# Linear attention and two MLP layers on one core: phi as the stationary operand of the product with v, v with a column of ones, and the identity matrix made on VectorE

## The chip, the cores and the metric

The kernel runs on one core of a Trainium2 chip. Times are device microseconds (us) from the first to the last instruction of one execution and what lies around them; smaller is better. TensorE (PE, its weight loads PEld) multiplies matrices, VectorE (DVE) and ScalarE (ACT) work element by element, GpSimd (POOL) does what the others can't, and SyncE (SP) issues nearly all DMAs.

## What is computed

The reference, cut to what matters:

```python
# q, k, v: (4, 8, 576, 64)   w_phi: (64, 128)
def phi(x):
    proj = np.einsum('bhsd,df->bhsf', x, w_phi)
    proj = proj - np.max(np.abs(proj), axis=-1, keepdims=True)
    return np.concatenate([np.exp(proj), np.exp(-proj)], axis=-1)
q_p, k_p = (phi(q), phi(k))
kv = np.einsum('bhsf,bhsd->bhfd', k_p, v)
z = np.sum(k_p, axis=2)
num = np.einsum('bhsf,bhfd->bhsd', q_p, kv)
den = np.einsum('bhsf,bhf->bhs', q_p, z)[..., None] + 1e-06
x = num / den                                   # laid out as (2304, 512)
h = x @ w_in;  x = np.maximum(h, 0) ** 2 @ w_out            # d_ff 2048
out = (sigmoid(x @ w_gate) * (x @ w_val)) @ w_out2          # d_ff 1536
```

phi has 256 features for each position of a head: 128 of exp(proj) and 128 of exp(-proj). kv is, for each head, 256 x 64, and z the sum of phi over the positions.

## The kernel before, in words

**Attention** runs in 16 steps, one for each batch b and pair j of heads (e = 0, 1). The 576 positions of a head are four rows r of 128 and a rest of 64; the rests of two heads lie together in the tiles kr, vr and phr. TensorE transposes q and k by the identity matrix (trans_q, L292; trans_k, L285; trans_rem, L300), multiplies them by w_phi (proj_q, L313; proj_k, L334), and the features come from exp on ScalarE. The maximum over the features of q comes from GpSimd's all-reduce (L318), that of k from VectorE (L339). phi of k is the tile ph: 128 positions by r, u and 128 features, where u = 0, 1 is the half of the features.

kv(b, j) makes kv and z with the *positions* contracted. v is the stationary operand and phi the moving one (L360): 64 columns of the array hold v of one head, the other 64 those of the other, and 256 columns of phi pass, so the bank pk has v's 64 dimensions of both heads on its 128 rows. The sums z come from a second row of matmuls (L367) with 32 columns of ones as the stationary operand, in four groups of columns. num(b, j), the product with phi of q, needs the *features* on the rows. So kt is copied out of PSUM (L369, L370), kv_tr transposes it in three pieces (L377), and L379 copies the result to ks. num has a product for the denominators (L390, 32 equal columns of z) and one for the numerators (L397), and VectorE and GpSimd turn these into the quotients (L401 to L417).

Step n issues, in this order: the exponentials of n, the projections of n+1 (L334, L313), the transposes of n+2, kv of n, num of n-1, kv_tr of n, and the loads of n+3. Each engine works in the order in which the scheduler put its instructions. PSUM is a pool of eight banks that all of this shares. Before the first step, make_identity (masks.py) clears a tile and sets its diagonal on GpSimd; TensorE begins with eight warm-up matmuls of the identity (L245).

**Weights.** Between the steps, and in the block that follows, weights arrive as 8-byte words and are converted (weight, L105 to L118: three operations on VectorE, a square on ScalarE, one more on VectorE). convert1(k) does the k-th piece of the first layer's w_in and w_out and writes the result to HBM (L147, L133); ten pieces are converted during attention, the other 22 in the first block, at 7/4 a step.

**The first block of the first layer** (t = 0) has steps s = 0 to 17: h0_step makes 128 columns of the hidden layer (L517) and squares them in two parts, ghi and glo (L521, L523), and o1_step multiplies those by w_out (L538). The further blocks use sums of the pieces of w_in (Strassen's scheme, L590), which in_sums makes: it reads two converted pieces back from HBM (L176, into the tiles wf that the block's own weights use too), forms four sums on VectorE (sums, L163 to L166, one buffer s) and writes them to HBM (L167). It is called for i = 0 to 7 at s = 3, 5, ..., 17.

Of the kernel before, what the change touches and what calls it, by code (L numbers as in the profile page):

```python
# [9 lines left out]

F32 = mybir.dt.float32
# [3 lines left out]
ALU = mybir.AluOpType  # L15
# [5 lines left out]
def attention_moe_moe2(ctx, tc, q, k, v, w_phi, w_in, w_out, w_gate, w_val, w_out2, out):  # L21
# [62 lines left out]
    def col_src(w, c):  # L84
        return w[:, c * P:(c + 1) * P].rearrange("(j p) f -> p j f", p=P)
# [40 lines left out]
    def in_piece(c):  # L126
        q, r = divmod(c, 4)
        return half[2 * q + r % 2][:, r // 2]
# [15 lines left out]
    def convert1(k):  # L144
        o, c = order1[k]
        if o == "in":
            nc.sync.dma_start(out=in_piece(c), in_=weight(wpa, col_src(w_in, c)))  # L147
        else:
            park(("o1", c), weight(wpa, row_src(w_out, c)))
        done.add((o, c))  # L150

    done = set()
    gvd = [dr.tile([P, 2, NJ * P], F32, tag=f"gv{c}", name="gvd") for c in range(C2)]
# [3 lines left out]
    kept = {}  # L157

    def sums(a, b, dst):
        a11, a12, a21, a22 = a[:, :HF], a[:, HF:], b[:, :HF], b[:, HF:]  # L160
# [52 lines left out]
    with ExitStack() as actx:  # L213
# [16 lines left out]
        ones = cst.tile([P, 32], F32, name="ones")  # L230
        nc.vector.memset(ones, 1.0)
# [17 lines left out]
        def load_rem(b):  # L249
            kr = ld.tile([SR, H, D], F32, tag="kr", name="kr", bufs=1)  # L250
            nc.sync.dma_start(out=kr, in_=k[b, :, SM:S, :].rearrange("h p d -> p h d"))
            nat["kr", b] = kr
            vr = lv.tile([P, 2, 2, D], F32, tag="vr", name="vr", bufs=2)
            for a in range(2):
                nc.sync.dma_start(out=vr[a * SR:(a + 1) * SR].rearrange("p g e d -> p (g e) d"),
                                  in_=v[b, 4 * a:4 * a + 4, SM:S, :].rearrange("h p d -> p h d"))
            nat["vr", b] = vr

        def load(b, j):
            t = ld.tile([P96, 2, 6, D], F32, tag="q", name="q", bufs=3)  # L260
            nc.sync.dma_start(out=t, in_=q[b, 2 * j:2 * j + 2].rearrange("h (p r) d -> p h r d", r=6))
            nat["q", b, j] = t
            t = ld.tile([P, 2, 4, D], F32, tag="k", name="k", bufs=3)
            nc.sync.dma_start(
                out=t, in_=k[b, 2 * j:2 * j + 2, 0:SM, :].rearrange("h (p r) d -> p h r d", r=4))
            nat["k", b, j] = t
            t = lv.tile([P, 2, 4, D], F32, tag="vx", name="vx", bufs=3)
            nc.sync.dma_start(
                out=t, in_=v[b, 2 * j:2 * j + 2, 0:SM, :].rearrange("h (p r) d -> p h r d", r=4))
            nat["vx", b, j] = t  # L270

        tT = {}
# [70 lines left out]
            ph[key] = t  # L343

        kvs = {}
        kts = {}


        def kv(b, j):
            tr = ph["r", b]  # L350
            vx = nat["vx", b, j]
            vr = nat["vr", b]
            a, g = divmod(j, 2)
            sl = slice(a * SR, (a + 1) * SR)
            pk = bank(2 * F)
            pz = bank(F)
            for r in range(5):
                for e in range(2):
# [3 lines left out]
            for r in range(5):  # L362
                for e in range(2):
                    l, t = (ones, ph[b, 2 * j + e][:, r]) if r < 4 else (ones[sl], tr[sl, 2 * g + e])
# [3 lines left out]
            kt = sm.tile([P, 3, F], F32, tag="kvt", name="kvt", bufs=2)  # L368
            nc.scalar.activation(kt[:, 0:2].rearrange("p u f -> p (u f)"), pk, AF.Copy)  # L369
            nc.scalar.activation(kt[:, 2], pz, AF.Copy)  # L370
            kts[b, j] = kt

        def kv_tr(b, j):
            kt = kts[b, j]
            pt = bank(3 * P)
            for u in range(3):
                nc.tensor.transpose(pt[:, u * P:(u + 1) * P], kt[:, u], ident)  # L377
            ks = sm.tile([P, 3 * P], F32, tag="kvs", name="kvs", bufs=3)
            nc.scalar.activation(ks, pt, AF.Copy)  # L379
            kvs[b, j] = ks  # L380

        def num(b, j):
            ks = kvs[b, j]
            pd = bank(SH)
            for u in range(2):
                for e in range(2):
                    for i in range(2):
                        q = 32 * (2 * e + i)
                        o = 2 * P + 32 * (2 * e + u)
                        nc.tensor.matmul(pd[q:q + 32], lhsT=ks[:, o:o + 32], rhs=qx[b, 2 * j + e, i][:, u, :],  # L390
                                         start=u == 0, stop=u == 1)
            pn = [bank(SH) for i in range(2)]
            for i in range(2):
                for u in range(2):
                    for e in range(2):
                        o = u * P + e * D
# [58 lines left out]
        for n in range(B * NJ):  # L455
# [331 lines left out]
    for s in range(C1 + 2):  # L787
        if s < C1:
            fetch_for(s + ahead)
            h0_step(s)  # L790
            split_in(s + 1)
        if 1 <= s <= C1:
            split_out(s - 1)
        for i, k in ((C1 - 5, "B11"), (C1 - 4, "B21"), (C1 - 3, "T2"), (C1 - 1, "T3"), (C1 - 1, "T1"), (C1, "B22"), (C1, "T4")):
            if s == i:
                xop(1, k)
        if s >= C1 - 1:
            run_ahead(0, 5, 0 if s < C1 else 3)
        if s >= 2:
            o1_step(0, s - 2, ws.pop(("out", s - 2)))  # L800
        if s < C1:
            converts1(s)
        if s >= 3 and s % 2 and s <= C1 + 1:
            for i in range(C1 // 2):
                if i == (s - 3) // 2:
                    in_sums(i)

    for k, (at, fn, *args) in enumerate(acts):
        run_ahead(first[k], 11, 6)
        fn(*args)  # L810
        converts2(at)
# [30 lines left out]
```

## Time and profile before

| | |
|---|---|
| median of 3 runs | 1026.83 us (1023.62 to 1028.88) |
| profiled execution, own time | 1027.08 us |
| its span, first to last instruction | 1025.3 us |
| PE busy | 992.4 us (97%) |
| PEld / DVE / ACT / POOL busy | 870.3 / 746.6 / 601.0 / 109.4 us |
| mean granted clock of TensorE | 0.994 |
| DMA moved | 162.18 MB, mean 158 GB/s |

The profile is of one execution. Attention takes the first 204 us, the first block of the first layer the time to about 343 us, and the other blocks of both layers the rest. "Busy" is the time in which an engine worked on at least one instruction; TensorE's matmuls are pipelined and their ends modelled. "Idle before" is the time that an engine stood still before an instruction, with what ended it. The chain of work that ended last is followed back from the last instruction: at each step to what released it. The granted clock is a share of full speed.

### The profile page before, as it was taken

The numbers are of one execution on the slowest core, as the hardware profiler recorded it, in microseconds if no ns is written. First come the engines' busy times: TensorE is split into PE (matmuls) and PEld (weight loads), VectorE is DVE, ScalarE is ACT, GpSimd is POOL, SyncE is SP. The second block draws the span as 40 slices with busy tenths as digits, with TensorE's granted clock in tenths as the row PEclk, the third lists the DMA queues.
The fourth block names the chain that finished last, engine by engine and source line by source line (L and its number), as shares of the span: only waits on it lengthen the run. The fifth ranks groups of instructions, "written<-read, shape, count | busy, mean of one in ns | idle before, by whom it ended". The sixth has DMA issues, their size and how long they took to land.

```text
span 1025.3 us, 17544 instructions
## 1 busy us (share of the span) xinstructions
PE 992.4 (97%) x6488; PEld 870.3 (85%) x6488; DVE 746.6 (73%) x1283; ACT 601.0 (59%) x1081; POOL 109.4 (11%) x198
## 2 busy tenths in 40 slices
PE   5999999999999899999999999999999999999996
PEld 5666666599999799889998899998899988899985
DVE  4799999869875797887968869866566656566542
ACT  4988888546545487545875457654465544455431
POOL 3555665400000000000000000000000000000000
PEclk9999999999999899999999999999999999999999
DMA  8345421339876478457584565642354422544302
GB/s 225 103 142 153 144 92 46 124 119 352 286 270 211 160 246 267 154 167 243 187 282 160 175 187 175 198 139 73 89 158 133 125 93 62 154 133 124 103 13 61
DMA packets 117846, 162.18 MB, mean 158 GB/s; under 512 B 12928, under 2 KB 75008, under 8 KB 117760
## 3 DMA queue, kind: packets, MB, share of 16 engines
q1 hardware_dynamic: 117120, 160.20, 49.8%
q8 instruction: 51, 0.84, 0.3%
q10 hardware_dynamic: 640, 0.85, 0.2%
q14 instruction: 35, 0.29, 0.1%
HBM read 127.99 MB, written 33.03 MB: 157 GB/s over the span
## 4 chain that ended last, share of the span: by engine, by line
PE 85%; DVE 6%; DMA 4%; ACT 2%; issue 2%; POOL 0%; ACTq 0%; SPq 0%; POOLq 0%; DVEq 0%
PE d L590 37%; PE d L538 17%; PE d L694 15%; PE d L517 4%; PE a L360 3%; DMA wf<-wid 2%; PE a L397 2%; PE a L334 2%; PE a L367 1%; PE a L390 1%; PE a L313 1%; DMA st<-in_moe_w_in_dram 1%; PE a L292 1%; DVE km L339 1%; PE a L377 1%
## 5 line engine op out<-in xcount | busy, mean ns | idle before, releaser
L590 PE MATMUL d<-xs,hl 128*128 128x384 f32 x2184 | 385.5, 337 | 3.6 <-ACT c L596 3.6
L590 PEld LDWEIGHTS d<-xs,hl 128*128 128x128 f32 x2184 | 379.5, 188 | 6.7 <-ACT c L596 4.9
L139 DVE TENSOR_TENSOR hl<-wf,hl 128x512 fp32r<-128x512 f32 x282 | 192.5, 688 | 76.4 <-ACT hl L138 75.3
L138 ACT ACTIVATE hl<-wf 128x512 fp32r<-128x512 f32 x282 | 174.9, 625 | 94.4 <-PE d L590 47.5
L538 PE MATMUL d<-ghi,hl 128*128 128x256 f32 (+1 forms) x768 | 191.9, 340 | 0.0
L538 PEld LDWEIGHTS d<-ghi,hl 128*128 128x128 f32 x768 | 133.0, 190 | 16.4
L538 PE MATMUL d<-glo,hl 128*128 128x512 f32 (+1 forms) x384 | 130.0, 342 | 5.1 <-DVE glo L523 5.1
L694 PE MATMUL d<-hl,ghi 128*128 128x512 f32 x432 | 126.7, 395 | 0.0
L94 ACT ACTIVATE ghi<-G 128x768 fp32r<-128x768 f32 x48 | 40.7, 847 | 99.3 <-PE d L694 56.0
L694 PEld LDWEIGHTS d<-hl,ghi 128*128 128x128 f32 x432 | 80.9, 188 | 18.2
L97 DVE TENSOR_TENSOR glo<-G,ghi 128x768 fp32r<-128x768 f32 x48 | 46.0, 958 | 57.3 <-ACT ghi L94 56.9
L596 ACT ACTIVATE c<-d 128x768 f32<-128x768 f32 x78 | 61.3, 809 | 44.7 <-PE d L590 44.5
L318 POOL PARTITION_ALL_REDUCE m<-qe x64 | 82.5, 1359 | 28.5 <-ACT qe L316 26.8
L538 PEld LDWEIGHTS d<-glo,hl 128*128 128x128 f32 x384 | 73.1, 190 | 14.1 <-DVE glo L523 5.4
L619 DVE TENSOR_TENSOR c<-c,d 128x768 f32<-128x768 f32 x54 | 51.2, 953 | 41.1 <-ACT c L596 26.8
L694 PE MATMUL d<-hl,glo 128*128 128x512 f32 x216 | 76.3, 395 | 0.0
L517 PE MATMUL d<-xs,hl 128*128 128x384 f32 x384 | 69.2, 337 | 2.1 <-DVE u L417 1.7
L517 PEld LDWEIGHTS d<-xs,hl 128*128 128x128 f32 x384 | 66.6, 188 | 3.8 <-DVE u L417 2.2
L116 ACT ACTIVATE st<-st 128x512 f32<-128x512 f32 x68 | 45.7, 680 | 37.0 <-DVE w L113 34.2
L694 PEld LDWEIGHTS d<-hl,glo 128*128 128x128 f32 x216 | 40.6, 188 | 9.8
L113 DVE SCALAR_TENSOR_TENSOR w<-st,w 128x512 uint32<-128x512 uint32 x68 | 48.0, 718 | 0.3
L117 DVE SCALAR_TENSOR_TENSOR w<-st,w 128x512 f32<-128x512 f32 x68 | 46.3, 687 | 1.4 <-ACT st L116 0.5
(105 smaller groups left out, 1128.3 us busy)
## 6 DMA issues: line engine op xcount, KB each, us to landing
wf<-wd SPq DMA_DIRECT2D x84, 256.0 KB, 3.0
wf<-smd SPq DMA_DIRECT2D x72, 256.0 KB, 3.0
st<-in_moe_w_out_dram SPq DMA_DIRECT2D x28, 512.0 KB, 5.0
wf<-wid SPq DMA_DIRECT2D x56, 256.0 KB, 4.6
wf<-gvd SPq DMA_DIRECT2D x54, 256.0 KB, 3.1
st<-in_moe_w_in_dram SPq DMA_DIRECT2D x16, 512.0 KB, 5.1
wf<-ismd SPq DMA_DIRECT2D x32, 256.0 KB, 3.5
wd<-w SPq DMA_DIRECT2D x28, 256.0 KB, 3.3
```

Of the source, the lines that this page charges most:

```text
L97: last_g[0] = nc.vector.tensor_tensor(lo, src, f(hi), ALU.subtract)
L113: nc.vector.scalar_tensor_tensor(b, hi, 0xC0000000, b, ALU.bitwise_and, ALU.bitwise_or)
L117: nc.vector.scalar_tensor_tensor(a, h, TINY, a, ALU.is_ge, ALU.mult)
L138: nc.scalar.activation(d[:, 0], a, AF.Copy)
L139: nc.vector.tensor_tensor(d[:, 1], a, f(d[:, 0]), ALU.subtract)
L318: nc.gpsimd.partition_all_reduce(m, a[:, 1, :], channels=P, reduce_op=bass_isa.ReduceOp.absmax)
L517: nc.tensor.matmul(pp[:, i, :n], lhsT=w[:, x, j, :], rhs=xs[j][:, y, o:o + n], start=k == 0, stop=k == 3 * NJ - 1)
L538: nc.tensor.matmul(acc[j][i], lhsT=w[:, x, j, :], rhs=a[y][:, o:o + n], start=c == 0 and k == 0 and (i == 0 or j % 2 == 0), stop=c == C1 - ...
L590: nc.tensor.matmul(acc[k, q][:, m], lhsT=w[:, i, 2 * m + kt, :], rhs=v[:, j, kt, :], start=start and n == 0, stop=n == 5, skip_group_check ...
L596: nc.scalar.activation(side[name, q], acc["X", q], AF.Copy)
L619: nc.vector.tensor_tensor(a, a, acc[k, q], ALU.add)
L694: nc.tensor.matmul(acc[u], lhsT=g[x][:, u * P:(u + 1) * P], rhs=w[:, y].rearrange("p j f -> p (j f)"), start=c == 0 and n == 0, stop=c == ...
```

## The change

kv takes phi as the stationary operand, 128 positions by 128 features, and v as the moving one: 64 dimensions and a column of ones, 65 columns. The result has the features on its rows at once, kv in 64 columns and z in the 65th, for each head e and half u: one bank of 4 x 65 columns, 20 matmuls, one copy to ks. kv_tr, the product with ones and the two copies to kt are gone; num reads z with a step of 0 as 32 equal columns. For the ones, the tiles vx and vr get a 65th column, which GpSimd fills after each allocation, so v's DMAs write 256 bytes at a time, and vx has one DMA for each head. The identity comes from VectorE: a ramp by doubling, its transpose, a comparison, and four copies of a 32 x 32 block. And convert1 makes the sums of two pieces of w_in straight from the converted tiles, for the pieces that are converted after attention (five of the eight pairs); in_sums is called for the other three, at s = 2, 4 and 6.

```diff
     def convert1(k):
         o, c = order1[k]
         if o == "in":
-            nc.sync.dma_start(out=in_piece(c), in_=weight(wpa, col_src(w_in, c)))
+            a = weight(wpa, col_src(w_in, c))
+            nc.sync.dma_start(out=in_piece(c), in_=a)
+            kept[c] = a
+            if k >= len(CONVERTING) and c % 2:
+                sums(kept[c - 1], a, wsm[c // 4][:, :, c % 4 // 2])
+                done.add(("sum", c // 2))
...
         ident = cst.tile([P, P], F32, name="ident")
-        make_identity(nc, ident)
+        ramp = cst.tile([P, 3, 32], F32, name="ramp")
+        nc.vector.memset(ident, 0.0)
+        nc.vector.memset(ramp[:, 0, 0:1], 0.0)
+        for n in (1, 2, 4, 8, 16):
+            nc.vector.tensor_scalar(ramp[:, 0, n:2 * n], ramp[:, 0, :n], float(n), None, ALU.add)
+        nc.vector.transpose(ramp[:, 1], ramp[:, 0])
+        nc.vector.tensor_tensor(ramp[:, 2], ramp[:, 0], ramp[:, 1], ALU.is_equal)
+        for i in range(4):
+            sl = slice(32 * i, 32 * i + 32)
+            nc.vector.tensor_copy(ident[sl, sl], ramp[sl, 2])
...
-            t = lv.tile([P, 2, 4, D], F32, tag="vx", name="vx", bufs=3)
-            nc.sync.dma_start(
-                out=t, in_=v[b, 2 * j:2 * j + 2, 0:SM, :].rearrange("h (p r) d -> p h r d", r=4))
+            t = lv.tile([P, 2, 4, D + 1], F32, tag="vx", name="vx", bufs=3)
+            nc.gpsimd.memset(t[:, :, :, D:], 1.0)
+            for e in range(2):
+                nc.sync.dma_start(
+                    out=t[:, e, :, :D], in_=v[b, 2 * j + e, 0:SM, :].rearrange("(p r) d -> p r d", r=4))
...
-            pk = bank(2 * F)
-            pz = bank(F)
+            pk = bank(4 * (D + 1)).rearrange("p (e u d) -> p e u d", e=2, u=2)
             for r in range(5):
                 for e in range(2):
-                    l, t = (vx[:, e, r, :], ph[b, 2 * j + e][:, r]) if r < 4 else (vr[sl, g, e, :], tr[sl, 2 * g + e])
-                    nc.tensor.matmul(pk[e * D:(e + 1) * D], lhsT=l, rhs=t.rearrange("p u f -> p (u f)"),
-                                     start=r == 0, stop=r == 4)
...
                     for u in range(2):
-                        o = 32 * (2 * e + u)
-                        nc.tensor.matmul(pz[o:o + 32], lhsT=l, rhs=t[:, u], start=r == 0, stop=r == 4)
...
-        def kv_tr(b, j):
...
-                nc.tensor.transpose(pt[:, u * P:(u + 1) * P], kt[:, u], ident)
-            ks = sm.tile([P, 3 * P], F32, tag="kvs", name="kvs", bufs=3)
-            nc.scalar.activation(ks, pt, AF.Copy)
+                        l, t = (ph[b, 2 * j + e][:, r, u], vx[:, e, r]) if r < 4 else (tr[sl, 2 * g + e, u], vr[sl, g, e])
+                        nc.tensor.matmul(pk[:, e, u], lhsT=l, rhs=t, start=r + e + u == 0, stop=r == 4, skip_group_check=True)
+            ks = sm.tile([P, 2, 2, D + 1], F32, tag="kvs", name="kvs", bufs=3)
+            nc.scalar.activation(ks, pk, AF.Copy)
...
-                        nc.tensor.matmul(pd[q:q + 32], lhsT=ks[:, o:o + 32], rhs=qx[b, 2 * j + e, i][:, u, :],
+                        nc.tensor.matmul(pd[q:q + 32], lhsT=ks[:, e, u, D:].to_broadcast([P, 32]), rhs=qx[b, 2 * j + e, i][:, u, :],
...
-                        nc.tensor.matmul(pn[i][e * D:(e + 1) * D], lhsT=ks[:, o:o + D],
+                        nc.tensor.matmul(pn[i][e * D:(e + 1) * D], lhsT=ks[:, e, u, :D],
...
-            kv_tr(b, j)
...
-        if s >= 3 and s % 2 and s <= C1 + 1:
-            for i in range(C1 // 2):
-                if i == (s - 3) // 2:
-                    in_sums(i)
-
+        if s in (2, 4, 6, 8) and ("sum", s // 2 - 1) not in done:
+            in_sums(s // 2 - 1)
```

The order of instructions shows two places. The first is TensorE in one whole attention step, here the kernel before, from the transposes of one step to those of the next (a is a PSUM bank; a matmul here is two instructions in the profile, a transpose one):

```order
L292 MATMUL a<-ident,q 128x96 x6
L285 MATMUL a<-ident,k 128x128 x4
L360 MATMUL a<-ph,vx 64x256 x8
L360 MATMUL a<-phr,vr 64x256 x2
L367 MATMUL a<-ph,ones 32x128 x16
L367 MATMUL a<-phr,ones 32x128 x4
L390 MATMUL a<-qe,kvs 32x288 x8
L397 MATMUL a<-qe,kvs 64x288 x8
L377 MATMUL a<-ident,kvt 128x128 x3
L334 MATMUL a<-wk,kT 128x256 x12
L313 MATMUL a<-qT,wq 128x288 x12
```

And the same step of the changed kernel, whose line numbers differ (L306 and L299 transpose q and k, L371 is kv, L383 and L389 are num, L348 and L327 the projections):

```order
L306 MATMUL a<-ident,q 128x96 x6
L299 MATMUL a<-ident,k 128x128 x4
L371 MATMUL a<-vx,ph 128x65 x16
L371 MATMUL a<-vr,phr 128x65 x4
L383 MATMUL a<-qe,kvs 32x288 x8
L389 MATMUL a<-qe,kvs 64x288 x8
L348 MATMUL a<-wk,kT 128x256 x12
L327 MATMUL a<-qT,wq 128x288 x12
```

The product with ones and the three transposes of kvt are gone, and kv has 20 matmuls with 65 columns in place of 10 with 256.

The second is VectorE at the end of the first block, before (hl and glo are low parts that TensorE waits for, s the sums, c a difference of x for the next block):

```order
L139 TENSOR_TENSOR hl<-wf,hl 128x512
L523 TENSOR_TENSOR glo<-c,ghi 128x768
L139 TENSOR_TENSOR hl<-wf,hl 128x512
L163 TENSOR_TENSOR s<-wf 128x256
L165 TENSOR_TENSOR s<-wf 128x256
L164 TENSOR_TENSOR s<-s,wf 128x256
L166 TENSOR_TENSOR s<-wf,s 128x256
L163 TENSOR_TENSOR s<-wf 128x256
L165 TENSOR_TENSOR s<-wf 128x256
L164 TENSOR_TENSOR s<-s,wf 128x256
L139 TENSOR_TENSOR hl<-wf,hl 128x512
L166 TENSOR_TENSOR s<-wf,s 128x256
```

And the changed kernel around the last glo (L514) of the block:

```order
L138 TENSOR_TENSOR hl<-wf,hl 128x512
L514 TENSOR_TENSOR glo<-c,ghi 128x768
L552 TENSOR_TENSOR c<-u 128x768
L552 TENSOR_TENSOR c<-u,c 128x768
L138 TENSOR_TENSOR hl<-wf,hl 128x512
L96 TENSOR_TENSOR xs<-c,xs 128x768
L138 TENSOR_TENSOR hl<-wf,hl 128x512 x2
L514 TENSOR_TENSOR glo<-c,ghi 128x768
L138 TENSOR_TENSOR hl<-wf,hl 128x512 x2
L514 TENSOR_TENSOR glo<-c,ghi 128x768
L552 TENSOR_TENSOR c<-u 128x768
```

The sums s from wf, between the last two glo before, are no longer there; in the changed kernel they stand earlier, most of them with w, the converted tile, as their source.

## Rows read from the trace of the kernel before

**Rows 1.** By stage: stretch, length, busy PE, PEld, DVE, ACT, POOL; clock, DMA.

```profile
0.00:9.76 9.76, 0.00 (x0) 0.00 (x0) 2.17 (x12) 1.28 (x1) 0.68 (x6) 1.00 0.86 218
...
57.39:138.01 80.62, 80.01 (x918) 52.50 (x917) 75.25 (x166) 68.28 (x168) 47.36 (x85) 1.00 0.49 146
138.01:161.57 23.56, 23.20 (x266) 15.27 (x264) 21.77 (x49) 19.18 (x48) 13.31 (x25) 1.00 0.26 81
...
204.26:343.10 138.84, 133.41 (x759) 124.49 (x759) 100.77 (x177) 70.12 (x104) 0.00 (x0) 0.99 0.72 239
343.10:347.90 4.80, 4.80 (x15) 4.12 (x16) 4.49 (x6) 3.09 (x4) 0.00 (x0) 0.51 0.90 308
```

**Rows 2.** Timeline of the start: start us, us, instruction, count, idle before.

```profile
1.06 0.63 DVE L237 CAST wk<-zr 128x128 fp32r<-128x128 f32 x4
...
9.43 0.28 POOL masks.py:199 TENSOR_SCALAR_AFFINE_SELECT ident<-ident 128x128 f32<-128x128 f32 x1 [8.51 <-issue]
...
9.76 3.74 PE L245 MATMUL a<-ident 128*128 128x128 f32 x16 [9.76 <-POOL ident masks.py:199]
...
13.34 0.66 PE L292 MATMUL a<-ident,q 96*128 96x96 f32 x6
...
16.00 4.95 POOL L318 PARTITION_ALL_REDUCE m<-qe  x4 [6.29 <-ACT qe L316]
```

**Rows 3.** Chain of work that ended last, in one step: start us, us, what.

```profile
68.73 2.46 PE a L360 x20
71.19 1.36 PE a L367 x40
...
75.75 0.48 PE a L377 x3
76.23 1.40 PE a L334 x12
...
79.48 0.49 PE a L285 x4
79.98 2.46 PE a L360 x20
```

**Rows 4.** Timeline at the end of the first block, of DVE and of PE.

```profile
333.83 0.43 DVE L163 TENSOR_TENSOR s<-wf 128x256 f32<-128x256 f32 x1 [4.00 <-DMA wf<-wid]
...
339.54 0.42 DVE L163 TENSOR_TENSOR s<-wf 128x256 f32<-128x256 f32 x1 [4.16 <-DMA ismd<-s]
...
343.10 0.80 PE L538 MATMUL d<-glo,hl 128*128 128x512 f32 x1 [5.07 <-DVE glo L523]
```

**Rows 5.** Groups by form, 0 to 180 us, small DVE operations: busy, mean ns.

```profile
L404 DVE RECIPROCAL rd<-rd 128x9 f32<-128x9 f32 x13 | 2.8, 216 | 0.4
...
L403 DVE TENSOR_SCALAR rd<-den 128x9 f32<-128x9 f32 x13 | 2.1, 163 | 0.1
```

**Rows 6.** DMA issues: KB, median us to landing; last, early q loads.

```profile
vx<-in_v_dram SPq DMA_DIRECT2D x16, 256.0 KB, 3.1
...
vr<-in_v_dram SPq DMA_DIRECT2D x8, 64.0 KB, 2.8
...
DMA to landing us min/median/max: 2.9/4.6/5.9
```

**Rows 7.** Groups by form, 0 to 180 us, weight loads: busy, mean ns.

```profile
L334 PEld LDWEIGHTS a<-wk,kT 128*128 128x128 f32 x180 | 22.4, 188 | 1.8 <-ACT kT L276 1.4 <-DVE kT L277 0.3 <-issue 0.2
...
L360 PEld LDWEIGHTS a<-ph,vx 128*64 128x64 f32 x224 | 14.8, 136 | 8.1 <-ACT qT L276 0.8 <-issue 0.5 <-ACT ph L341 0.3
...
L367 PEld LDWEIGHTS a<-ph,ones 128*32 128x32 f32 x448 | 11.5, 109 | 5.8 <-issue 2.3 <-DVE qT L277 1.5 <-ACT ph L342 0.8
...
L285 PEld LDWEIGHTS a<-ident,k 128*128 128x128 f32 x64 | 6.9, 140 | 0.2
...
L245 PEld LDWEIGHTS a<-ident 128*128 128x128 f32 x16 | 3.5, 330 | 9.8 <-POOL ident masks.py:199 9.8
```

**Rows 8.** Timeline at the end of attention, of PE.

```profile
199.25 1.18 PE L390 MATMUL a<-qe,kvs 128*32 128x288 f32 x16 [0.58 <-ACT kvs L379]
```

More of the change, by code (lines that the diff above doesn't have):

```diff
@@ L6 @@
 from concourse import mybir
-from concourse.masks import make_identity
 from concourse._compat import with_exitstack
@@ L152, in attention_moe_moe2 @@
     done = set()
+    kept = {}
     gvd = [dr.tile([P, 2, NJ * P], F32, tag=f"gv{c}", name="gvd") for c in range(C2)]
@@ L156, in attention_moe_moe2 @@
     order2 += [(c, 2) for c in range(C2)]
-    kept = {}
     def sums(a, b, dst):
@@ L229, in attention_moe_moe2 @@
         split(wq[:, 0], wq[:, 1], wst)
-        ones = cst.tile([P, 32], F32, name="ones")
-        nc.vector.memset(ones, 1.0)
         zr = cst.tile([P, F], F32, name="zr")
@@ L252, in load_rem @@
             nat["kr", b] = kr
-            vr = lv.tile([P, 2, 2, D], F32, tag="vr", name="vr", bufs=2)
+            vr = lv.tile([P, 2, 2, D + 1], F32, tag="vr", name="vr", bufs=2)
+            nc.gpsimd.memset(vr[:, :, :, D:], 1.0)
             for a in range(2):
-                nc.sync.dma_start(out=vr[a * SR:(a + 1) * SR].rearrange("p g e d -> p (g e) d"),
+                nc.sync.dma_start(out=vr[a * SR:(a + 1) * SR, :, :, :D].rearrange("p g e d -> p (g e) d"),
                                   in_=v[b, 4 * a:4 * a + 4, SM:S, :].rearrange("h p d -> p h d"))
@@ L345, in attention_moe_moe2 @@
         kvs = {}
-        kts = {}
         def kv(b, j):
@@ L354, in kv @@
             sl = slice(a * SR, (a + 1) * SR)
-            pk = bank(2 * F)
-            pz = bank(F)
+            pk = bank(4 * (D + 1)).rearrange("p (e u d) -> p e u d", e=2, u=2)
             for r in range(5):
                 for e in range(2):
-                    l, t = (vx[:, e, r, :], ph[b, 2 * j + e][:, r]) if r < 4 else (vr[sl, g, e, :], tr[sl, 2 * g + e])
-                    nc.tensor.matmul(pk[e * D:(e + 1) * D], lhsT=l, rhs=t.rearrange("p u f -> p (u f)"),
-                                     start=r == 0, stop=r == 4)
-            for r in range(5):
-                for e in range(2):
-                    l, t = (ones, ph[b, 2 * j + e][:, r]) if r < 4 else (ones[sl], tr[sl, 2 * g + e])
-                    for u in range(2):
-                        o = 32 * (2 * e + u)
-                        nc.tensor.matmul(pz[o:o + 32], lhsT=l, rhs=t[:, u], start=r == 0, stop=r == 4)
[L368 to L371, printed above, removed]
-        def kv_tr(b, j):
-            kt = kts[b, j]
-            pt = bank(3 * P)
-            for u in range(3):
-                nc.tensor.transpose(pt[:, u * P:(u + 1) * P], kt[:, u], ident)
-            ks = sm.tile([P, 3 * P], F32, tag="kvs", name="kvs", bufs=3)
-            nc.scalar.activation(ks, pt, AF.Copy)
+                    for u in range(2):
+                        l, t = (ph[b, 2 * j + e][:, r, u], vx[:, e, r]) if r < 4 else (tr[sl, 2 * g + e, u], vr[sl, g, e])
+                        nc.tensor.matmul(pk[:, e, u], lhsT=l, rhs=t, start=r + e + u == 0, stop=r == 4, skip_group_check=True)
+            ks = sm.tile([P, 2, 2, D + 1], F32, tag="kvs", name="kvs", bufs=3)
+            nc.scalar.activation(ks, pk, AF.Copy)
             kvs[b, j] = ks
@@ L388, in num @@
                         q = 32 * (2 * e + i)
-                        o = 2 * P + 32 * (2 * e + u)
-                        nc.tensor.matmul(pd[q:q + 32], lhsT=ks[:, o:o + 32], rhs=qx[b, 2 * j + e, i][:, u, :],
+                        nc.tensor.matmul(pd[q:q + 32], lhsT=ks[:, e, u, D:].to_broadcast([P, 32]), rhs=qx[b, 2 * j + e, i][:, u, :],
                                          start=u == 0, stop=u == 1)
@@ L395, in num @@
                     for e in range(2):
-                        o = u * P + e * D
-                        nc.tensor.matmul(pn[i][e * D:(e + 1) * D], lhsT=ks[:, o:o + D],
+                        nc.tensor.matmul(pn[i][e * D:(e + 1) * D], lhsT=ks[:, e, u, :D],
                                          rhs=qx[b, 2 * j + e, i][:, u, :], start=u == 0, stop=u == 1)
@@ L802, in attention_moe_moe2 @@
             converts1(s)
-        if s >= 3 and s % 2 and s <= C1 + 1:
-            for i in range(C1 // 2):
-                if i == (s - 3) // 2:
-                    in_sums(i)
+        if s in (2, 4, 6, 8) and ("sum", s // 2 - 1) not in done:
+            in_sums(s // 2 - 1)
+    kept.clear()
     for k, (at, fn, *args) in enumerate(acts):
```

## The prediction, made before the changed kernel was run

> **What bounds the kernel now.** I read the table by stage first. TensorE is the engine to watch: it idles for the first 9.76 us, is busy 80.01 of 80.62 us in the middle of attention, and 133.41 of 138.84 us in the first block of the first layer [rows 1]. So three places can move: the start, the attention steps and the end of that block. After 347.9 us TensorE has no idle time that this change touches, and I leave that part as it is.
>
> In the timeline of the start TensorE's first instruction, the warm-up of line 245, waits 9.76 us for the identity, which GpSimd finishes with an affine select at 9.43 us after 8.51 us in which nothing that the profile shows ran on it [rows 2].
>
> In the chain of one attention step (head pair) TensorE's own instructions follow each other. From one product with v to the next it is 79.98 - 68.73 = 11.25 us [rows 3]. What TensorE does is then paid in full, unless VectorE ends the step: it is busy 21.77 of 23.56 us in one later stretch [rows 1].
>
> At the end of the block, TensorE's row at 343.10 us shows 5.07 us of idle time before the last product of the block, for the low part glo. VectorE made glo late since it works in order and stood 4.00 and 4.16 us before the sums of lines 163 to 166, once for a piece read back from HBM, once for the buffer that the previous sums were being written from [rows 4]. In the 4.80 us behind that idle time the granted clock is 0.51, the lower of TensorE's levels [rows 1].
>
> **The change, part by part.**
>
> *Start.* Thirteen small VectorE instructions replace the GpSimd pair. The nearest rows are operations on 9 columns, 163 and 216 ns [rows 5]; I take 0.19 us each, 2.5 us. Clearing zr and the four casts of line 237 (0.63 us in all) stand between them, some 0.8 us, so from VectorE's first work at 0.80 us the identity is there at 4.1 us (3.6 to 4.5 by the two rows). The warm-up then takes as long as before, 13.34 - 9.76 = 3.58 us [rows 2], so the first transposes of q stand at 7.7 us and not 13.34. That is **-5.6 us** if nothing else is late. Next in line: the data, and GpSimd's all-reduce. q is there: a load of q lands 2.9 to 5.9 us after its issue [rows 6], and the first is issued below 1 us. The first all-reduce started at 16.00 us, on its data [rows 2]; it would be wanted at 10.4 us. Its code may need as long as the affine select did, 8.51 us from about 1 us on: 10 us, so it just fits. GpSimd's memsets of the ones columns are short and stand ahead of that.
>
> The v loads are now in pieces of 256 bytes, two issues for one, on a queue that was 86% busy until 9.76 us [rows 1]. A load of vr, in such pieces, took 2.8 us for 64 KB, one of vx 3.1 us for 256 KB [rows 6]; that bounds the price between nothing and four times, and both are mostly latency. I take nothing for the sum, as the second pair's q is transposed only after the first pair's projections, and keep 2.5 us for the range: **-3 to -6.2 us**. The Trainium skill's page "DMA: Bandwidth & Descriptors", section "Specifications", says that transfers under 512 bytes fall below line rate by a read-modify-write. If that doubled the three first v loads (0.79 of some 2.66 MB), data would come 30% later and the start would lose about 1 us, a sum of 1019.2; no row of this trace shows v in such pieces. In the later steps the queue is half idle (DMA share 0.49), and the price is nothing.
>
> *Attention step.* Removed: 20 matmul instructions of line 360 (2.46 us on the chain), 40 of line 367 (1.36), 3 transposes of line 377 (0.48), together 4.30 us [rows 3]. They ran two or four side by side in columns of the array. Added: 20 matmuls, each two instructions as all float32 ones here, 40 pairs of a 128-wide load of phi and a matmul over 65 columns of v, one after another. Which half sets the pace? The load: two float32 loads that differ by 32 columns took 136 and 109 ns [rows 7], 0.84 ns a column, 0.108 us for 128; the matmul has 65 columns. The nearest rows for the pair are the 16 warm-up pairs with a 128-wide float32 load: 3.58 us, 0.224 each [rows 2]. Their loads took 330 ns where other 128-wide loads took 188 [rows 7], so although the column of the granted clock reads 1.00 there, I read the lower level, 1.2 GHz, and halve it: 0.112. The other end is line 334, with 128-wide loads: 12 in 1.40 us, 0.117 [rows 3]. So **0.112, ends 0.108 and 0.117**. Three transposes of kvt took 0.48 us, four of k 0.49 [rows 3], so a change of operand shape costs some 0.12 us; two of them are left. A step then has 40 x 0.112 + 0.24 = 4.72 us in place of 4.30: **+0.42 us**, between +0.26 and +0.62. For 14 steps that is +5.9 us. I take off 0.8 us for four steps that VectorE ends (half of 0.42 absorbed in each) and 0.6 us at the last step, where TensorE waited 0.58 us for the copy of the transposed kv [rows 8]: that wait goes, since num(14) now covers the only copy. **+4.5 us, between +2 and +7.5.** The three ScalarE copies that become one are off the path. The ones columns' memset waits on GpSimd for the kv that frees its buffer, and the copies of rd and the next all-reduce queue behind it; both need matmuls that follow that kv on TensorE, so nobody waits longer. den comes from the same eight matmuls as before.
>
> *Sums of the first layer.* The order of VectorE shows five of the eight sums now made from pieces still in SBUF, and the three read-back ones early; none is left among the last steps of the block. Ten reads of 256 KB go from SyncE's queue. So the 5.07 us go, and with them the slow clock: 4.80 x (1 - 0.51) = 2.4 us; 7.5 us in all. What could be late next is VectorE's other work in the block: it was busy 100.77 of 138.84 us [rows 1], and three sums (some 5 us) move forward into the part where the weights are converted. That fits. **-7.5 us, between -3 and -8.**
>
> **The sum.** 1027.08 - 5.6 + 4.5 - 7.5 = 1018.5 us against the profiled execution's own time. The median of the runs, 1026.83 us, is 0.25 below that, so I forecast **1018.2 us**.
>
> **Rivals.**
>
> *Loads that don't hide.* If a 128-wide load cannot go on beside the short matmul before it, a pair costs 0.112 + 0.057 (65 columns, half of the warm-up's 128) = 0.169 us, a step 7.0 us, +2.7 each and about +36 us in all; the time would be about **1050 us**. The change loses as soon as a pair takes more than 0.127 us, where 14 steps eat the 13.1 us gained elsewhere. Against it: 16 warm-up pairs took 0.224 us each with load and matmul equally wide, which is one of the two, not the sum. The Trainium skill's page "TensorE: Matmul & The Clock Gate", in Part 3 under "What overlaps and what doesn't", says that a weight load overlaps running matmuls only where its row group differs. All of phi's loads use all rows, so by that rule this rival would hold; the warm-up rows speak against the rule here. Chance 0.06.
>
> *Loads at half the price.* A transposed 128-wide load took 140 ns, not 188 [rows 7]. If phi's loads were like that, a pair would take 0.064 us, a step 2.8, and the time would be about 991 us. Against it are the two float32 loads above, which are of phi's kind. Chance 0.04.
>
> *The stall at the end of the block stays.* VectorE, with more sums in the converting part, or a wait for the weights' own loads, makes glo late elsewhere. Then 1018.2 + 7.5 = 1025.7 us. Against it: VectorE had 38 us free there. Chance 0.12.
>
> *The start is bound by loads or by GpSimd's code.* Then it gives 3 us and not 5.6: 1020.8 us. Chance 0.10.
>
> **How the numbers follow.** My forecast has 0.68, the rivals the rest. The main case alone runs from about 1014 to 1024 us by its bounds (-6.2 + 2 - 8 and -3 + 7.5 - 7.5, with the ends seldom together). To leave out no more than 2 in 10 I take in the rivals at 1020.8 and 1025.7 us: **1012 to 1027 us**. About 0.5% is what a measurement of this kernel can tell from no change, 5.1 us, so faster means below 1021.7. The main case lies there in 17 of 20, the start rival in rather more than half, the half-price one surely: 0.66. The rest of these and the stall rival are the same: 0.26. Loads that don't hide, and a bad end of several bounds: 0.08.
>
> **What would show it.** Right: the first transposes of q at 7 to 8 us; line 371's 40 pairs in 4.3 to 4.8 us and a step of 11.5 to 12 us in place of 11.25; no transposes of kvt; no idle time over 1 us on TensorE between the first product of the block and line 590's counterpart, and no clock of 0.5 there. Wrong: a pair of line 371 over 0.127 us or under 0.10; a first all-reduce that starts later than its data; TensorE waiting for glo or hl between 210 and 340 us.

## The result and the profile of the changed kernel

The changed kernel takes 1016.68 us (median of 4 runs, 1015.71 to 1016.94), the one before 1026.11 beside it (4 runs, 1023.62 to 1028.88): a ratio of 0.9906, 95% interval 0.9879 to 0.9933. The forecast was 1018.2 us, range 1012 to 1027. The profiled execution took 1015.71 us with a span of 1013.9, so 11.4 us less than the profiled one before.

The table by stage of the changed kernel, stretches as in [rows 1]: the start, seven attention steps (the 4th to the 11th product with v, as before), and 139.55 us from the first product of the block on. Before, TensorE stood 5.07 us ahead of 343.10 us and had the block's last products done at about 349.0 us; here they are done at about 337.3, so the third stretch reaches a little into the next block. Columns: stretch, length, busy PE, PEld, DVE, ACT, POOL; clock, DMA.

```profile
0.00:9.76 9.76, 6.10 (x44) 5.58 (x44) 5.72 (x28) 3.51 (x7) 0.62 (x10) 1.00 0.91 202
51.63:135.29 83.66, 83.16 (x758) 66.82 (x756) 75.52 (x166) 65.39 (x154) 48.59 (x94) 1.00 0.49 141
201.05:340.60 139.55, 139.55 (x801) 131.01 (x800) 109.67 (x191) 76.73 (x113) 1.30 (x8) 1.00 0.69 232
```

TensorE works 6.10 us of the first 9.76, in which it had stood all the time. In attention it is as full as before and takes 83.66 us for what took 80.62. In the third stretch it has no idle time at all, and the clock stays at its upper level; VectorE, busy 109.67 us, still has room.

The timeline of the start, of DVE, PE and POOL (start us, us, instruction, count, idle before), answers to [rows 2]:

```profile
2.88 0.73 DVE L237 COPY ident<-ramp 32x32 f32<-32x32 f32 x4
...
3.66 3.48 PE L256 MATMUL a<-ident 128*128 128x128 f32 x16 [3.66 <-DVE ident L237]
...
6.98 0.66 PE L306 MATMUL a<-ident,q 96*128 96x96 f32 x6
...
9.60 4.91 POOL L332 PARTITION_ALL_REDUCE m<-qe  x4 [8.62 <-ACT qe L330]
```

The identity is there at 3.66 us in place of 9.76, the first transposes of q start at 6.98 in place of 13.34, and the all-reduce waits for its data from ScalarE, not for GpSimd.

The chain of one step (start us, us, what) answers to [rows 3]:

```profile
63.24 4.55 PE a L371 x40
67.79 1.11 PE a L383 x16
68.90 2.09 PE a L389 x16
70.99 1.61 PE a L348 x12
...
74.46 0.49 PE a L299 x4
74.95 1.15 PE a L371 x10
```

The 40 pairs of line 371 take 4.55 us (4.55 to 4.79 over the steps) where lines 360, 367 and 377 took 4.30; the projections of k behind them take 1.61 and not 1.40; the change of operand shape that stood at the transposes of kvt now stands there, which is a reading of the order and not tested. The step is 11.71 us, and was 11.25.

The loads of line 371 (view of one line: duration ns min/median/max) are of the kind that the prediction took them for:

```profile
L371 PEld LDWEIGHTS a<-vx,ph x512: 186/192/192, 17.6 to 193.4; 128*128 128x128 f32 x171
```

At the end of attention TensorE used to wait. The first product of the block, in the timeline of PE before:

```profile
204.26 2.02 PE L517 MATMUL d<-xs,hl 128*128 128x384 f32 x10 [1.74 <-DVE u L417]
```

and in the changed kernel, with no wait:

```profile
201.05 3.21 PE L508 MATMUL d<-xs,hl 128*128 128x384 f32 x17
```

With the starts of the products with v from the timelines (before: first 24.12, last 190.28, last numerator done at 202.52, block at 204.26; after: 17.70, 189.91, 201.05, 201.05) and the one idle time that both kernels have later, 0.90 us at 487.41 before and 475.79 after, the account is (the two rows are of PE, before and after):

```profile
488.31 6.86 PE L590 MATMUL d<-xs,hl 128*128 128x384 f32 x38 [0.90 <-ACT c L596]
...
476.69 18.64 PE L581 MATMUL d<-xs,hl 128*128 128x384 f32 x106 [0.90 <-ACT c L587]
```

| stretch | before | after | change | predicted |
|---|---|---|---|---|
| start, to the first product with v | 24.12 | 17.70 | -6.42 | -5.6 |
| 15 steps | 166.16 | 172.21 | +6.05 | +5.1 |
| last step, to its last matmul | 12.24 | 11.14 | -1.10 | -0.6 |
| wait ahead of the block | 1.74 | 0 | -1.74 | not seen |
| block, to the common idle time | 283.15 | 274.74 | -8.41 | -7.5 |

Together -11.6 us; the rest of the program gives back 0.2.

### The profile page after: what moved, and what is told of

Its sections match the earlier page's. It is cut to its first block, busy times and chain, and to the rows that moved or that the text cites. A ratio compares the mean times of both kernels' runs of the same rounds, so it can differ in the third digit from the quotient of the medians.

```text
span 1013.9 us, 16814 instructions
## 1 busy us (share of the span) xinstructions
PE 996.2 (98%) x6120; PEld 901.6 (89%) x6120; DVE 748.0 (74%) x1295; ACT 594.4 (59%) x1049; POOL 111.5 (11%) x216
## 4 chain that ended last, share of the span: by engine, by line
PE 98%; ACT 1%; DVE 0%; ACTq 0%; issue 0%
PE d L581 38%; PE d L529 20%; PE d L685 15%; PE a L371 7%; PE d L508 7%; PE a L389 3%; PE a L348 3%; PE a L383 2%; PE a L327 1%; PE a L306 1%; PE a L299 1%; ACT qe L330 0%; PE a L256 0%; ACT c L587 0%; DVE c L694 0%; ACTq L698 0%
## 5 line engine op out<-in xcount | busy, mean ns | idle before, releaser
L371 PE MATMUL a<-vx,ph 128*128 128x65 f32 x512 | 59.8, 275 | 0.2 <-issue 0.2
L371 PEld LDWEIGHTS a<-vx,ph 128*128 128x128 f32 x512 | 58.4, 192 | 1.3 <-issue 0.8
```

The lines of the kernel that those rows point to most:

```text
L371: nc.tensor.matmul(pk[:, e, u], lhsT=l, rhs=t, start=r + e + u == 0, stop=r == 4, skip_group_check=True)
```

## The experiments

The theory was that three independent parts add up, with a new product that costs 0.4 us a step because a 128-wide load of phi sets its pace. The rivals: gains that are given back or need each other, and a pair that is something other than one load. Ratios are against the kernel before, run beside each.

**Identity alone.** Edit: the 13 VectorE instructions for the GpSimd identity, nothing else.

```diff
-        make_identity(nc, ident)
+        ramp = cst.tile([P, 3, 32], F32, name="ramp")
...
+            nc.vector.tensor_copy(ident[sl, sl], ramp[sl, 2])
```

> The kernel before with the identity made on VectorE and nothing else. Theory (three parts that add up): the first transposes of q move from 13.34 to about 7.0 us, everything behind them comes 6.4 us earlier, and the whole is 6.0 to 6.6 us shorter than before, near 1020.3 us. Rival (the start is given back): the first steps of attention wait for loads, VectorE or the all-reduce, or the stall of 5.07 us at the end of the block grows, since the weights' loads come no earlier; the whole gains 3 us or less.

Measured: 1020.76 us (6 runs) against 1027.04, ratio 0.9938 (0.9925 to 0.9950): 6.3 us less. The stall at the end of the block is 4.79 us and doesn't grow. Unexpected: the wait of 1.74 us ahead of the block is gone here too, though the attention step is that of before. So the 6.3 us are not the start alone. The first product with v comes at 19.14 us, 4.98 earlier and not 6.42: six transposes of q behind the warm-up took 1.17 us here and 0.66 in the changed kernel. And 0.67 us come back at the first pair, where TensorE stands 1.41 us before the transposes of kvt and stood 0.74 before (group of PE before, to 180 us: busy, mean ns, idle before and its releaser):

```profile
L377 PE MATMUL a<-ident,kvt 128*128 128x128 f32 x40 | 8.1, 293 | 0.7 <-ACT kvt L369 0.7
```

**Sums alone.** Edit: five sums from pieces in SBUF, three read back early.

```diff
+            kept[c] = a
+            if k >= len(CONVERTING) and c % 2:
+                sums(kept[c - 1], a, wsm[c // 4][:, :, c % 4 // 2])
...
-        if s >= 3 and s % 2 and s <= C1 + 1:
+        if s in (2, 4, 6, 8) and ("sum", s // 2 - 1) not in done:
```

> The kernel before with the sums of the first layer made from the pieces in SBUF and the three others early, and nothing else. Theory (three parts that add up): no idle time of TensorE before the last products of the block and no stretch at the clock of 0.51, 8.5 us less than before (7.5 to 9), near 1018.3 us. Rival (the stall is only moved): VectorE runs late elsewhere, and the gain is 4 us or less. The wait of 1.74 us for u ahead of the first product of the block stays by the theory; where it goes here too, it was not the attention step that removed it.

Measured: 1019.50 us (6 runs), ratio 0.9922 (0.9909 to 0.9936), 7.5 us less. TensorE is busy for the whole of the block, and the wait of 1.74 us for u stays. The table by stage of this kernel, from the first product of the block:

```profile
204.90:344.45 139.55, 139.55 (x799) 131.00 (x800) 108.24 (x188) 76.75 (x113) 0.00 (x0) 1.00 0.69 232
```

**The new product alone.** Edit: phi stationary and the column of ones; identity and sums as before.

```diff
-                    nc.tensor.matmul(pk[e * D:(e + 1) * D], lhsT=l, rhs=t.rearrange("p u f -> p (u f)"),
-                                     start=r == 0, stop=r == 4)
...
+                        nc.tensor.matmul(pk[:, e, u], lhsT=l, rhs=t, start=r + e + u == 0, stop=r == 4, skip_group_check=True)
```

> The kernel before with phi stationary and the column of ones, the identity still from GpSimd and the sums still read back. Theory (three parts that add up): the first 15 steps together take 6.0 us more, the end of the last step to the first product of the block 2.8 us less, so 3.3 us slower than before (2.5 to 4.5), near 1030.2 us. Rival A (the end is not its doing): the 2.8 us at the last step come from the sums or the start, and this is 6 us slower. Rival B (the steps are not its doing): the whole stays within 1 us of before, or below it.

Measured: 1032.99 us (6 runs), ratio 1.0056 (1.0043 to 1.0069), 5.95 us slower and not 3.3. Rival A had the number right, but not its reason: the last step does give its 1.0 us here, and the wait behind it is what differs. The 15 steps take 172.35 us, as in the changed kernel, so the steps' price is the product's; but the wait ahead of the block (timeline of PE) has grown:

```profile
209.61 1.75 PE L495 MATMUL d<-xs,hl 128*128 128x384 f32 x6 [2.81 <-DVE u L396]
```

**All but the new product.** Edit, in the changed kernel: the attention step of before.

```diff
-                        nc.tensor.matmul(pk[:, e, u], lhsT=l, rhs=t, start=r + e + u == 0, stop=r == 4, skip_group_check=True)
+                    nc.tensor.matmul(pk[e * D:(e + 1) * D], lhsT=l, rhs=t.rearrange("p u f -> p (u f)"),
+                                     start=r == 0, stop=r == 4)
```

> The changed kernel with the product of before in attention: identity on VectorE and the new sums, v stationary, ones and three transposes as before. Theory (three parts that add up): 6.4 + 8.5 = 14.9 us less than before, near 1012 us, and 3 to 5 us less than the changed kernel. Rival (they interact): part of what the identity or the sums give needs the new product (the wait of 1.74 us for u, GpSimd's all-reduce at the start), and the time is 1015 us or more.

Measured: 1013.13 us (4 runs), ratio 0.9863 (0.9849 to 0.9878): 13.9 us less than before, and 6.3 + 7.5 = 13.8 were to be expected from the first two. Those two add up, there is no wait ahead of the block, and the new product costs 1016.68 - 1013.13 = 3.55 us on top of them. The two kernels ran at different times: by their ratios it is 4.4 us, by the profiled executions 2.8. One group of this kernel (PE to 35 us: busy, mean ns, idle before and its releaser) shows what the old step has at the first pair with the early start:

```profile
L390 PE MATMUL a<-ident,kvt 128*128 128x128 f32 x3 | 0.8, 309 | 1.4 <-ACT kvt L382 1.4
```

**The bank.** By the kernel's text the product of line 517 doesn't read that u: its x comes from an earlier split. Its accumulator has two banks; if they cover the one that the last numerators are still read from, it has to wait. Edit, in the kernel before: the warm-up in two banks.

```diff
-        warm = bank(P)
-        for _ in range(NWARM):
+        for i in range(NWARM):
+            if i % (NWARM // 2) == 0:
+                warm = bank(P)
```

> The kernel before with the warm-up's eight matmuls written to two banks of the accumulator in place of one. Every engine's order of instructions stays the same; only the rotation of the eight banks moves by one, so that the first product of the block no longer writes where the last step of attention is still being read. Theory (the wait of 1.74 us for u ahead of that product is the bank's): it goes, and the whole is 1.7 us shorter than before, 1.3 to 2.0. Rival (it waits for u as data, or the next product waits as long): no change.

Measured: 1025.54 us (12 runs) against 1027.28, ratio 0.9977 (0.9968 to 0.9986): 1.74 us less. With every engine's order unchanged the wait is gone (timeline of PE):

```profile
201.17 2.16 PE L398 MATMUL a<-qe,kvs 128*64 128x288 f32 x16
203.26 3.04 PE L518 MATMUL d<-xs,hl 128*128 128x384 f32 x16
```

So the 1.74 us belong to none of the change's parts by its purpose. Which bank the block starts in follows from how the rotation happens to stand. The identity's edit removed the wait and two kernels below, which also have that identity, have one of 2.8 us again; what turns the rotation in each was not taken apart. The same edit in the kernel with the new product alone:

> The kernel before with phi stationary and the column of ones alone, and the warm-up written to two banks, so that the banks of attention rotate by one with every engine's order of instructions kept. Theory (2.8 us of what this product cost alone were the wait for the bank at the first product of the block): that wait goes, and the whole is 2 to 2.8 us less than without the rotation, near 1030.4 us, 3.4 us over before; the new product's own price is then the same 3.3 to 3.6 us with the other two parts and without them, apart from the wait of 1.74 us that before has. Rival (the two or three first products wait for u in any bank): 1032.5 us or more.

Measured: 1030.06 us (12 runs), ratio 1.0025 (1.0015 to 1.0035), 2.9 us less than without it. A wait of 0.72 us for u is left at the second accumulator. Against the kernel before with the same rotation (1025.54) the product then costs 4.5 us, 0.72 of it that wait: 3.8 us, within the 2.8 to 4.4 that it costs beside the other parts.

**Is the pair one load?** Edit, in the changed kernel: tiles of v with 128 columns, and all of them moved.

```diff
-            pk = bank(4 * (D + 1)).rearrange("p (e u d) -> p e u d", e=2, u=2)
+            pk = bank(4 * P).rearrange("p (e u d) -> p e u d", e=2, u=2)
...
-            t = lv.tile([P, 2, 4, D + 1], F32, tag="vx", name="vx", bufs=3)
+            t = lv.tile([P, 2, 4, P], F32, tag="vx", name="vx", bufs=3)
```

> The changed kernel with 63 more columns of ones behind v, so that line 371's matmul moves 128 columns in place of 65 behind the same load of phi; the extra products are not read. Theory (the load runs beside the matmul before it and sets the pace): a pair stays at 0.112 us, at most 0.117, since the warm-up's pairs of a 128-wide load and 128 columns took 0.224 at the lower clock; the whole stays within 3 us of the changed kernel, 1016 to 1020 us. Rival (0.112 is a load at half price and the matmul, one after the other: 0.055 + 0.057): a pair takes 0.055 + 0.112 = 0.167 us, 40 x 16 pairs add 35 us, near 1052 us.

Measured: 1023.75 us (5 runs), ratio 0.9966 (0.9952 to 0.9980): above the theory's 1016 to 1020 and far under the rival's 1052. The line and the chain say which holds:

```profile
L371 PE MATMUL a<-vx,ph x512: 275/275/377, 19.6 to 198.4; 128*128 128x128 f32 x171
...
65.80 4.75 PE a L371 x40
```

Almost twice the columns cost 0.1 to 0.2 us in 40 pairs: 0.119 a pair and not 0.167, so the matmul is hidden beside the load. Most of the 7 us over the changed kernel are elsewhere: the wait for u ahead of the block is back (2.83 us), and the first product with v is 1.95 us later, 0.88 of it since the identity comes at 4.54 us. The 15 steps take 3.0 us more, 1.8 of it in the pairs. VectorE's first small operations, beside GpSimd's larger memsets, take longer than in the changed kernel; whether the memsets are the cause wasn't tried.

**Place or read.** Edit, in the kernel with the new sums alone: the sums in the same places, from pieces read back.

```diff
-                sums(kept[c - 1], a, wsm[c // 4][:, :, c % 4 // 2])
+                done.add((o, c))
+                in_sums(c // 2)
```

> The kernel before with the sums in the changed kernel's places, right behind the conversion of their second piece, but all eight from pieces read back from HBM. Theory P (the place is what counts): VectorE waits a few us more for each piece in a part where it has 33 us free, TensorE does not, and the gain is that of the sums alone, 7 to 8 us, near 1019.5 us. Theory D (the read is what counts): VectorE stands in front of what TensorE needs next, TensorE idles 1 us or more in several places between 210 and 340 us, and the gain is 4 us or less.

Measured: 1040.97 us (4 runs), ratio 1.0134 (1.0118 to 1.0149): 21.5 us slower than with the pieces kept. Theory D's loss, but in the traces not by way of VectorE's order. The timeline of SP, ACT and PE:

```profile
228.87 0.32 SPq L148 DMA_DIRECT2D wid<-w  x1
229.28 0.38 SPq L182 DMA_DIRECT2D wf<-wid  x1
...
231.56 0.42 SPq L203 DMA_DIRECT2D wf<-wid  x1
...
236.77 1.15 ACT L138 ACTIVATE hl<-wf 128x512 fp32r<-128x512 f32 x2 [3.87 <-DMA wf<-wid]
...
237.45 1.01 PE L523 MATMUL d<-xs,hl 128*128 128x384 f32 x2 [6.98 <-ACT hl L138]
```

The store of a fresh piece (line 148) waits for its conversion (10.4 us in three waits of the queue from 215 to 300 us), the read of it (line 182) stands behind the store, and the weights that TensorE needs next (line 203) behind both in SyncE's queue. TensorE stood 6.98, 4.76 and 1.91 us that way. Behind such waits the clock falls too: 0.94 on average here (table by stage, from the first product of the block), where it was 1.00 with the pieces kept.

```profile
205.11:345.00 139.89, 125.49 (x679) 116.40 (x680) 95.96 (x171) 65.16 (x94) 0.00 (x0) 0.94 0.73 239
```

So the new places alone don't give the gain; with the reads they lose. No run keeps the pieces and leaves the sums at the end of the block, so what the kept pieces give without the new places is not shown.

**The new product where it pays.** Edit: phi stationary in the first and the last pair, the product of before in the other fourteen.

```diff
-            kv(b, j)
+            (kv if (b, j) in NEW else kv_old)(b, j)
...
+            if (b, j) not in NEW:
+                kv_tr(b, j)
```

> The changed kernel with phi stationary in the first and the last head pair alone, and the product of before in the other fourteen. Theory (the new product costs 0.4 us in a step whose transposes of kvt are covered, and pays where they are not: at the last pair, where TensorE waited 0.58 us for their copy, and at the first, where the kernel with the product of before idled 1.41 us ahead of them): 1.0 us from the last pair and 0.5 to 1 us from the first, against 1013.1 us of the kernel with the product of before everywhere: 1011.1 to 1011.8 us, 5 us less than the changed kernel. Rival (those waits move on to the next step): 1013 us or more.

Measured: 1010.25 us (4 runs), ratio 0.9834 (0.9820 to 0.9847), 2.9 us less than without the new product and 0.9 below the theory's 1011.1. Neither 1.41 nor 0.58 us of idle time is left, and the block starts at 196.01 us where it started at 198.23. It beats both kernels.

**Halves of the load.** If the load sets the pace, its width is what to change. Edit, in the changed kernel:

```diff
-                        nc.tensor.matmul(pk[:, e, u], lhsT=l, rhs=t, start=r + e + u == 0, stop=r == 4, skip_group_check=True)
+                        for h in (slice(0, 64), slice(64, P)):
+                            nc.tensor.matmul(pk[h, e, u], lhsT=l[:, h], rhs=t, start=r + e + u == 0, stop=r == 4, skip_group_check=True)
```

> The changed kernel with each 128-wide load of phi made as two loads of 64 columns, each with its own matmul over the same 65 columns of v, into the upper and the lower half of the accumulator's rows: 80 pairs of instructions a step for 40, the same columns loaded. Theory A (a load's pace is its columns, 0.84 ns each by the loads of 128 and 32 columns, and halves go one after the other): a pair takes 0.054 to 0.06, 80 of them 4.3 to 4.8 us as the 40 did, the whole within 4 us of the changed kernel. Theory B (each instruction has a price of its own): a pair takes 0.07 us or more, 5.6 us a step, 14 us slower or more. Theory C (halves of the array load side by side): 80 pairs take 2.3 to 3 us, the steps shorten by 1.5 us or more until VectorE ends them, and the whole is 10 us or more faster.

Measured: **992.84 us** (4 runs), ratio 0.9661 (0.9640 to 0.9682), 24 us less than the changed kernel. Theory C. Its timeline of PE, one step, and then a stretch of almost seven steps in the table by stage:

```profile
67.34 2.09 PE L372 MATMUL a<-vx,ph 128*64 128x65 f32 x64
69.36 0.68 PE L372 MATMUL a<-vr,phr 64*64 64x65 f32 x16
...
67.34:138.00 70.66, 69.24 (x1029) 52.21 (x1030) 69.56 (x165) 61.15 (x151) 47.62 (x89) 1.00 0.52 142
```

Twice as many pairs take 2.63 us on the chain, 0.033 each, where 40 took 4.55. The mean step falls from 172.21 / 15 = 11.5 us to 9.8 (15 steps in 146.33), and now TensorE (69.24 of 70.66 us) and VectorE (69.56) are both nearly always busy: the chain of work runs through VectorE up to 87.19 us and mostly through TensorE behind that. Is it the halves that stand side by side, or are short loads cheap in themselves? The same 80 pairs in another order tell it:

```diff
-            for r in range(5):
-                for e in range(2):
-                    for u in range(2):
...
+            for h in (slice(0, 64), slice(64, P)):
+                for r in range(5):
+                    for e in range(2):
+                        for u in range(2):
```

> The kernel with 64-column loads and the same 80 pairs a step, in another order: the 40 matmul instructions into the lower half of the array's columns first, then the 40 into the upper half, where the other took the halves in turn. Theory C1 (a load and its matmul run beside the neighbour's only where that stands in the other half of the columns): a pair takes 0.054 to 0.06 us again, 80 of them 4.3 us or more, and the whole is near that of the changed kernel, 1012 us or more. Theory C2 (a load of 64 columns behind a matmul of 65 is cheap by itself, whatever stands before it): 80 pairs take 2.6 us as with the halves in turn, and the whole stays within 4 us of that kernel, 989 to 997 us.

Measured: 1033.77 us (6 runs), ratio 1.0066 (1.0046 to 1.0086), 41 us slower for an order. The chain has 5.23 us for the 80 pairs, 0.065 each, a little above the 0.054 to 0.06 of theory C1, which holds in kind; theory C2 does not. The timeline of PE:

```profile
67.52 2.08 PE L372 MATMUL a<-vx,ph 128*64 128x65 f32 x32
69.53 0.68 PE L372 MATMUL a<-vr,phr 64*64 64x65 f32 x8
70.14 2.08 PE L372 MATMUL a<-vx,ph 128*64 128x65 f32 x32
72.15 0.68 PE L372 MATMUL a<-vr,phr 64*64 64x65 f32 x8
```

32 pairs in one half of the columns take 2.08 us, and with the halves in turn 64 pairs take 2.09: a second pair in the other half is free. (2.81 us of the 41 are a wait for u ahead of the block.)

## Why the prediction was right, and by which terms

*What bounds it.* Right: TensorE's own time in attention, and the three places were the ones that moved.

*Start, -5.6.* Measured -6.4. The identity came at 3.66 us and not 4.1: VectorE's 18 instructions up to there, the clearing of zr and four casts among them, were 2.57 us of busy time where 3.3 had been put. The warm-up took 6.98 - 3.66 = 3.32 us to the next instruction, not 3.58. That is luck of this execution and not the change: with the same identity it took 3.58 again in the traces of the identity alone, of all but the new product and of the halves, and the first product with v stood at 19.14, 18.13 and 18.09 us there. The all-reduce started at 9.60 us on its data: the guess that GpSimd's code might need 8.51 us again was harmless, and no run shows how long it needs. The 256-byte pieces of v cost nothing that shows: TensorE waits for no load at the start, and the first product with v is at 17.70 and 18.09 us with them (changed kernel, halves) and at 18.13 without (all but the new product).

*Attention, +4.5.* The price of the pair is right: 0.112 predicted, 0.114 to 0.120 measured, 4.55 to 4.79 us for 40 against 4.48. That it is one load beside a hidden matmul is shown by the run with 128 columns. Two terms were mis-sized. The steps give +6.05 in all where 5.9 - 0.8 was put, for 14 steps though 15 lie between the first and the last product with v. The mean, +0.40 a step against +0.42, is nearer than its parts: ten of the 15 grew by 0.44 to 0.67 us, 0.55 on average, and five by -0.21 to 0.27. So a full step costs more than was put, and more than 0.8 us is absorbed; which engine absorbs it was not taken apart. The last step gave 1.10 us and not 0.6: besides the wait of 0.58 us its three transposes of kvt (0.55) are gone from the path. One term was missing: the 1.74 us ahead of the block, which made the total +3.2. It is in the same view as [rows 8], and was not taken apart because its releaser reads as data; it was a bank. That it fell away is luck, as no part of the change is made for it.

*End of the block, -7.5.* Measured -8.4 here and in the trace of the sums alone (274.74 us to the common idle time), 7.5 between the medians there. The stall and the slow stretch went. Besides the 5.07 us the block held 0.36 us of other idle time (busy 133.41 of 138.84 us [rows 1]), which the sum left out. The cause given, VectorE standing before the read-back pieces and the buffer, is read from [rows 4] and fits the sums alone, but no run isolates it: the run that kept the reads at the new places lost TensorE's time in SyncE's queue, of which the prediction had said only that ten reads go.

*The rivals.* Loads that don't hide are excluded: 32 of a step's 40 loads of phi use all 128 rows, as their matmuls do, and a pair takes 0.114 us, with 128 columns 0.119. The Trainium skill's page "TensorE: Matmul & The Clock Gate", Part 3, "What overlaps and what doesn't", has a load overlap only where its row group differs; the measurement decides against it here. Loads at half the price are excluded for 128 columns (192 ns in the row, 0.114 a pair), but the time that this rival gave, 991 us, was there to be had in another way, by halving them: 992.84. The two numbers agree by accident: the rival had one cheaper load, and what gave the time is two loads of half the width side by side. The stall that stays and the start that is bound did not happen.

*The reach of the sum.* The terms erred by -0.8, +1.0, -0.5, -1.7 and -0.9 us, some 3.0 in all and most of them to the same side, of which the rest of the program gives back 0.2: 1015.71 us in the profiled execution against a sum of 1018.5. The median lies 0.97 above the profiled one, so the forecast was 1.5 us over.

## What to carry to other kernels

Where a matmul moves few columns, as 65 behind a load of 128 here, its weight load sets the pace, so count the columns loaded, not the columns moved; then split the load over halves of the array's columns and take the halves in turn. A small change elsewhere can shift which accumulator bank the next stage opens with: a wait whose releaser reads the bank's old content and makes none of the operands may be for the bank, and shifting the rotation by one bank tests it. A change of three parts is best run in its parts: here two gained 13.9 us, and the third cost some 3.5 of them.

## What the runs showed of the hardware that was not expected

Pairs of a 64-column load and a 65-column matmul take 0.065 us each in one half of the columns and 0.033 with the halves in turn. In the prediction line 360's pairs, also 64 wide and in turn, told nothing of it: with 256 moving columns a pair took 0.123 us [rows 3]. But line 367's row there held it, 40 pairs of a 32-wide load and 128 moving columns in 1.36 us, 0.034 each, in four groups of columns in turn. The Trainium skill's page "TensorEngine Tiling (Array Packing)", section "Key Properties", says that different tiles can execute loads and matmuls in parallel; 64 pairs in 2.09 us against 32 in 2.08 agree. What would lie below 0.033, with VectorE out of the way, is open: quarters of 32 columns weren't run.
